# Attention and mixture of experts in one kernel: tail masks over all rows, gate halves exchanged on GpSimd, another order of every engine

## The chip, the core and the metric

The kernel runs on one core of a Trainium2 chip. A core has five engines that run their own instruction queues: TensorE (PE; its weight loads are listed apart as PEld), VectorE (DVE), ScalarE (ACT), GpSimd (POOL) and SyncE (SP), which here only issues DMAs. Engines wait for each other through semaphores, and each works strictly through its own queue: an instruction that waits holds all that stand behind it. The metric is the device time of one execution, in microseconds.

## The reference, cut to what matters

Eight batches of 576 positions. First, attention with 8 heads of 64 in a causal window of 128 positions with a linear bias:

```
rel = pos[:, None] - pos[None, :]
scores = scale * q @ k.T - slope[h] * abs(rel)
attn = softmax(where((rel >= 0) & (rel < 128), scores, -1e9)) @ v
```

The heads' results, side by side, are `x` (576 x 512 for each batch). Then a mixture of four experts, each one a causal attention of width 64 over `x`:

```
logits = x @ w_gate; the two largest of four are kept, w = softmax of these two
for e in range(4):
    y_e = softmax(causal(scale * (x @ wq[e]) @ (x @ wk[e]).T)) @ (x @ wv[e]) @ wo[e]
    out += where(e is kept, w, 0) * y_e
```

## The kernel before

Heads are worked in pairs: a batch has four pairs `g`, each with its heads in partitions 0 to 63 and 64 to 127 of one tile. 576 rows are four blocks of 128 and a tail of 64. For a pair, `attn_s` (line 401) multiplies scores on PE into PSUM, DVE masks and biases them and takes the row minimum of the negated scores (`softmax_block`, a custom DVE instruction), ACT exponentiates with a running sum (`exp_block`), DVE sums and inverts, and POOL or ACT scales the rows (`normalise`, line 467). PE then turns the blocks by transposes against an identity (`attn_t`), and multiplies with v (`attn_pv`). The result is split into a rounded part and a remainder (`rnd`, `ssub`), so that the projections run in the fast float32 form on three products. For each batch, `vproj` (687) makes the experts' values and the gates' logits `lg`, `gates` (726) the gate weights `w`, `qkproj` the queries and keys, `moe_s`, `moe_norm` (835), `moe_t` and `moe_pv` the experts' attention, `moe_wo` the output.

The first four pairs of batch 0 take another road: `fetch` (329) brings only their first 256 rows at first ("the first row fetches": eight DMAs of 128 KB, two for each pair), `first_blocks` scores them against tables `FT` (the tile `KKm` in the rows), and `half_s`, `half_tail` (527) and `half_t` do the rest later. The tables are made at the start from `tbt` (one DMA on ACT's queue) by DVE and POOL. Before that data comes, PE runs eight matmuls on a zeroed tile (`warm`, `AHTm` in the rows).

Two odd exchanges of partition halves run through this: in blocks with odd number, `moe_s` puts the lower 64 rows into the upper partitions. So the logits of odd blocks are copied to `lg` in two halves by DVE (lines 721 to 724), and the tail's gate weights are copied by DVE in `moe_norm` to a column `r[:, 1:2]`. The tail mask `mkt[:, P:]` serves the 64-wide tail blocks, one half of partitions at a time (425, 426).

The order of the work is not that of the code. Everything is recorded first; then `plan` (199) reads `ORDER`, a packed list of numbers, and emits the recorded operations in that order, on every engine; where an operation has two forms (`evac`: ACT or DVE; `rnd`: POOL or ACT; `scl`: POOL or ACT; `ssub`: DVE or POOL) the number also chooses one. `place` then gives the tiles their slots by first use. All instructions are therefore booked to line 1225.

Of the kernel before, what the change touches and what calls it, by code (L numbers as in the profile page):

```python
# [21 lines left out]
E = 4  # L22
# [21 lines left out]
    "4BG=Sx4)*E2XVv$_q7D_SSbM{5}U6*3L>dE25bs}Sx%=UH<17azeXiC}}(8OW2{ld|E3?<P9F@b}Bj2*dCUA_o8?C8J#`8ZU`Xso5QF$;<4$bGPOM(I05;"
    "sfR>JMVW~ysl=1$xt&_De-H^8s1AK)dZa{+pVtz}wO!eR(_DBEKrU^*2mA=CX$G50FYO<Ka2)5nv`yn1XtD#*6ub4=E+A@UG0u-}ug}i0VH<Iu20Os_>>B"
    "zexg%>y#wu<gG?xT*fCt59c`B-coVKJQS@?X@t{$#txLV{IXNo5%)Qvq^?Rx-;DUb}Xxt;(W?Dk%O9_a1^8pOS&?B2IO_lZx1yYwe7CPgcQ<iHlXdBOAL9"
    "{`-bvI-ETCVH}x)^Q$vzi-!c4Jm3EzIwL$MzgbcjTAro;>&M_#3m^(yfY;3%THAr@qzS$Rt*gWKm6$XUjEbz(pN%V@)h%wa;N~fP<_EXEqMB4J*Ok$lv@g"
    "e13ik!d;j#pN?ygK%5GKswYF`ikkJ6UvGBB(bnAN9ZIp{fwYWU+A6Y;7{eQpptCHNk8yDWp_==nE>}zj$P})jx7`YREi(j%iuU?JV-D$x{a}q^8BSU9fCP"
    "~Jf`<|Qxc0m>WsVIf$etvmJM)nJ$?&xfE3_}O%=vSpbe;nQo^8A%m0yd|7rmhj9w^J2cgNATLQ?0G*bO?~pW?g}%j$i%tl!DNmzRp~l<ygLYYI-U_%H+&s"
    "ml3ft33I#jH7(b_izWEr^GpByJFO$TD|gpB`_9%@-3|*1b2@F{B4^GP%`3fa$^=?m7**jFcx~V*^x^l2Nsyn@g-~nD5(=}O*6bm~8G#!JvD>gpavGaj);H"  # L50
    "lAgy_jQB?ild#8D2Q>ki^1%?G6=9$0j>oQXzzJLJj+Nx~WAM%=*q!t#{_859z~tdL+&vo^d3@=8)H<Us}{8nphoTJ+-&zVrf0``-6Uz8Du&5OE<k1gog06"
    "rhBcknTxME7+hZq5uP1e(8CUY;?0vEJP3(IDVOXWzc|$I5j?&*75P*)fZuI{P%vjuB`#I&uq2>Ol+>hBuo`%+X}PWYUris>Gg4NiQjgS{t~`EuyW%%^7PB"
    "dA(JcDWW}y5q3J1QQHG7N4kM|B8l{q5xc0{D>BB+vywkQ;ncN5uiF2SM24;jEAR|hN4t;Yrmi9$qY1jHl!NJ~*oU|+$h*+h3*cOFr+HUOK+P{Emw{*&9?H"
    "IE^ZruU07k>r1V7^6qk2E9^TfIILT+>OAcBf-<1$P%!Ifz}+?AnmiHtdiSGH3{%WDlf58|}w?Nw9V1prY?acHU;Hy96+%yilUZD>0D~8cO9GD6IhL6Zq9P"
    "1$gdGZEwr0)23j3A)_F#q-lh}=r3Nf5gE~4+a9zECu8c_Ef`=JZR}k9+aTAy>yha<_&O5~S*K+8Gby@%J2+Ie{qt*bkK=UAs3guPANY~yQBQ`ot~u%Qc^A"
    "p6i~xv?S%7(1K=jVVXuiNYM3+ks5|V|LIKYmq^muUEwBjOLc7IUGetgDa?oB9NSggGUq`E()^Fs9tiBF)~wdFO?6KGyxm-fW80tD=uyn<rT+No~z%J8<00"
    "4}b@!W(C58mVXv*vNEQaqR`bwq_ejb)vN~y>pC=SGWneV9PHoDUS;(I&GU!735N)Ya3iRYA`*uxgWaHqd!AFdp$Oxjs<&~<R;3h9Rrzy<l>>&L`j6qS^B}"
    "$IAy<qkwKU(%gUvQUC7IXN!gJLIk!u8+)KlPH1@e>>tjD4h~!63%}f?Urb7o>7Rp(Tw^twfDcBp_Y@s5^AZT2HQWy(@66qYQ08Hx+#_;s*C_wNUeBcYgSD"
    "+Z}C|5Qn6m*c4o|oGI({r#4aYTOF+Ox7qP+es?&Qf$oeiha7e}LuhqK{UVqOb1m!1ZfNap$%J-@LBiuy&>1(W|uK2HDmkH&mCWq|~*vwsb&wCDd#$osR99"
    "&aWXYRVr!gUFs**Kr<c#yl`iD^;iX>9{b7LKRq_6yPn#5033QE49=y*Qsif(B$6m+drL%T4(r`3m%kIsns~B1hP?LlzNaj2CEOF6zxN+6MNBW*GG@N<k@1"  # L60
    "A&B*i%kYn8$A)F*U+LB{EfigOFkra$>j1%C9shI0>v#iPln6!w`5(JW4?L<QPUo5a4@8y!`UG8wJpJo|=1`B9Ux<J7woiAK<fS~4;D^yg7U=@7d!&F!SWZ"
    "NSh=`*%6P5!;7iBHOk~%C;=6RNJWJR4EvWuFb>WozhYg|LUg*^+3iXXy1C6zyz%%0Yy)T#4>=D#TC%0h9=wQlj)LEx$Ttq<7VTc<Fa9u?s{aftRpKH%13H"
    "p?K7VodGY0JkP8*6c-WRZPY!g4)2$vLU2%i1OhMjBaV)fC9A(-N4g9yBwUyNnTM@Zd4OO*p2kLUuCa`O@8M+$>tIpig^h;L|gO0Mg1QX6M9GP@uk8E{C;l"
# [1249 lines left out]
```

## Time and profile before

| | |
|---|---|
| median of 3 runs | 476.78 us (476.32 to 477.31) |
| the profiled execution | 477.15 us, of which 475.4 us from its first to its last instruction |
| PE busy | 464.1 us, 98% |
| DVE, ACT, POOL busy | 400.8, 364.8, 240.9 us (84%, 77%, 51%) |
| matmuls and transposes on PE | 7100 |

The page cuts the span into 40 slices of 11.9 us; PE's row there is 7 tenths in the first, 6 in the last, and 9 in all between. The chain of work that ended last is made of PE for by far the greatest part. A time "us" at the start of a row counts from the first instruction of the program.

### The profile page before, as it was taken

The numbers are of one execution on the slowest core, as the hardware profiler recorded it, in microseconds if no ns is written. First come the engines' busy times: TensorE is split into PE (matmuls) and PEld (weight loads), VectorE is DVE, ScalarE is ACT, GpSimd is POOL, SyncE is SP. The second block draws the span as 40 slices with busy tenths as digits, with TensorE's granted clock in tenths as the row PEclk, the third lists the DMA queues.
The fourth block names the chain that finished last, engine by engine and source line by source line (L and its number), as shares of the span: only waits on it lengthen the run. The fifth ranks groups of instructions, "written<-read, shape, count | busy, mean of one in ns | idle before, by whom it ended". The sixth has DMA issues, their size and how long they took to land. (4 is left out here: it accounts for less than half of the span.)

```text
span 475.4 us, 18911 instructions
## 1 busy us (share of the span) xinstructions
PE 464.1 (98%) x7100; PEld 404.2 (85%) x7100; DVE 400.8 (84%) x1863; ACT 364.8 (77%) x1375; POOL 240.9 (51%) x449
## 2 busy tenths in 40 slices
PE   7999999999999999999999999999999999999996
PEld 4788889898789888898889988889789898799875
DVE  3899999989997798798997899797996899963972
ACT  3987898878989568687897958889789587743852
...
GB/s 148 288 198 221 173 90 110 6 26 114 21 263 90 3 59 134 156 103 55 56 128 30 142 27 83 252 9 1 161 99 56 36 75 30 91 1 1 4 90 134
DMA packets 28235, 44.75 MB, mean 94 GB/s; under 512 B 7664, under 2 KB 14192, under 8 KB 28144
## 3 DMA queue, kind: packets, MB, share of 16 engines
...
q14 instruction: 35, 0.29, 0.2%
...
## 5 line engine op out<-in xcount | busy, mean ns | idle before, releaser
L1225 ACT COPY w<-ps 128x512 f32<-128x512 f32 (+4 forms) x231 | 94.2, 452 | 43.7 <-PE ps L1225 33.4
L1225 ACT ACTIVATE w<-w,nm 128x128 f32<-128x128 f32 x252 | 98.8, 395 | 15.2 <-DVE nm L1225 13.5
L1225 PE MATMUL ps<-wx,WH 128*128 128x288 f32 (+2 forms) x512 | 107.5, 300 | 0.2
L1225 POOL TENSOR_SCALAR w<-w,mr,w 128x512 f32<-128x512 f32 (+3 forms) x128 | 77.8, 617 | 47.7 <-DVE mr L1225 22.6
L1225 POOL TENSOR_SCALAR w<-w,r 128x128 f32<-128x128 f32 (+1 forms) x166 | 61.8, 385 | 52.7 <-DVE r L1225 23.8
L1225 PEld LDWEIGHTS ps<-wx,WH 128*128 128x128 f32 x512 | 82.1, 189 | 2.7 <-DVE nm L1225 0.6
L1225 ACT ACTIVATE w<-w,mnm 128x384 f32<-128x384 f32 (+3 forms) x128 | 71.2, 558 | 6.4 <-DVE mnm L1225 6.4
L1225 DVE TENSOR_TENSOR w<-ps,tmt 128x768 f32<-128x768 f32 (+2 forms) x92 | 69.3, 776 | 4.8 <-PE ps L1225 4.6
L1225 DVE CUSTOM_DVE_ANT_0 w<-ps,tbt 128x128 f32<-128x128 f32 x272 | 68.5, 284 | 1.6
L1225 PE MATMUL ps<-w 64*64 64x128 f32 (+3 forms) x1200 | 65.8, 314 | 2.4 <-DMA w<-in_hd 2.4
L1225 PE MATMUL ps<-wx,WL 128*128 128x288 f32 (+2 forms) x256 | 67.3, 297 | 0.0
L1225 PE MATMUL ps<-idt,w 64*128 64x64 f32 (+1 forms) x1160 | 61.4, 231 | 2.9 <-POOL w L1225 2.1
L1225 PE MATMUL ps<-w,vt 64*64 64x192 f32 (+3 forms) x1344 | 60.5, 283 | 0.5 <-DMA vt<-in_vd 0.3
L1225 PEld LDWEIGHTS ps<-w 64*64 64x64 f32 x1200 | 49.4, 136 | 13.2 <-DMA w<-in_hd 4.5
L1225 DVE COPY w<-ps 128x128 f32<-128x128 f32 (+5 forms) x115 | 49.5, 451 | 12.9 <-PE ps L1225 11.2
L1225 PEld LDWEIGHTS ps<-idt,w 64*128 64x128 f32 (+1 forms) x1160 | 49.0, 139 | 13.3 <-POOL w L1225 5.6
L1225 PE MATMUL ps<-WH,wx 128*128 128x260 f32 x288 | 59.9, 289 | 0.0
L1225 PEld LDWEIGHTS ps<-w,vt 64*64 64x64 f32 (+1 forms) x1344 | 53.0, 133 | 6.6 <-issue 1.9
L1225 DVE COPY_PREDICATED ps<-mkt,ps 128x256 f32<-128x256 int32 (+3 forms) x180 | 53.4, 316 | 3.2 <-PE ps L1225 1.0
L1225 PE MATMUL ps<-w,w 64*64 64x64 f32 (+7 forms) x1088 | 53.0, 307 | 0.0
L1225 PE MATMUL ps<-KKm 64*64 64x288 f32 (+8 forms) x640 | 51.1, 411 | 0.0
L1225 ACT ACTIVATE w<-w,r 128x128 f32<-128x128 f32 (+1 forms) x122 | 44.0, 395 | 6.1 <-DVE r L1225 4.5
(107 smaller groups left out, 914.1 us busy)
## 6 DMA issues: line engine op xcount, KB each, us to landing
...
```

The costliest lines, as they stand in the source:

```text
L1225: getattr(getattr(tc.nc, e), m)(*a, **k)
```

## The change

The diff has five parts. The tail mask has two column blocks, one for each half of partitions with zeros in the other, so that a masked copy runs over all 128 partitions; `half_tail` has two such copies in place of one. The logits of odd blocks are copied straight, and the halves change places in the product that makes `w` (POOL, three instructions in place of one); the tail's logits are written in one half. `moe_norm` copies the tail's gate weights by POOL in place of DVE. A few POOL memsets zero what is no longer written. And `ORDER` is another list of numbers.

```
 ORDER = (
-    "c-o~|4_GBvb$>JWyt#LGW;4^wYu;<$i@XXA#N7xjSm*~46ch~4LWKkrT8K-82ph2AE)lw5A%PZjX+R-@f`WktTJQr47FtlKupdNFP*y?Nx}<Eg=+f-!Qdz"
...
+    "c-oCw4M1d9b)NU`nRoB*yzYDJJa<NCDx+XPK_P+xg$NZC5-^a0fw)AlprAv91{5kNC@3hTkbnUL1{4xds9?c>VGStQB>@8w6wH!9yK8q9Qr1Ar)?GvIeLw"
...
-    mkt = cp.tile([P, P + D], I32, name="mkt")
+    mkt = cp.tile([P, 2 * P], I32, name="mkt")
...
-            nc.vector.copy_predicated(s[:D, 3 * P : 3 * P + TAIL], mkt[:D, P:], s[:D, 2 * P + D : 3 * P])
-            nc.vector.copy_predicated(s[D:, 3 * P : 3 * P + TAIL], mkt[D:, P:], s[D:, P : P + D])
+            nc.vector.copy_predicated(s[:, 3 * P : 3 * P + TAIL], mkt[:, P : P + D], s[:, 2 * P + D : 3 * P])
+            nc.vector.copy_predicated(s[:, 3 * P : 3 * P + TAIL], mkt[:, P + D :], s[:, P : P + D])
...
-        nc.vector.copy_predicated(s[:, 0:TAIL], mkt[:, P:], s[:, P:TW])
+        for y in range(2):
+            nc.vector.copy_predicated(s[:, 0:TAIL], mkt[:, P + D * y : P + D * y + D], s[:, P:TW])
...
+        if t == 0:
+            nc.gpsimd.memset(lg[:, NQ, :], 0.0)
...
-            nc.vector.tensor_tensor(lg[D:P, t, :], acc[:D, E * D : n], tm2[:D, E * D :], add)
...
-        if t % 2:
-            for y in range(2):
-                nc.vector.tensor_copy(lg[D * y : D * y + D, t, :], acc[D - D * y : 2 * D - D * y, E * D : n])
-        else:
-            nc.vector.tensor_copy(lg[:, t, :], acc[:, E * D : n])
+        nc.vector.tensor_copy(lg[:, t, :], acc[:, E * D : n])
...
-        nc.gpsimd.tensor_tensor(
-            w.rearrange("p e t -> p t e"), ex, ws.unsqueeze(2).broadcast_to((P, n5, E)), mul
-        )
+        wt = w.rearrange("p e t -> p t e")
+        nc.gpsimd.tensor_tensor(wt[:, 0::2], ex[:, 0::2], ws[:, 0::2].unsqueeze(2).broadcast_to((P, 3, E)), mul)
+        for y in range(2):
+            a, z = slice(D * y, D * y + D), slice(D - D * y, 2 * D - D * y)
+            nc.gpsimd.tensor_tensor(wt[a, 1::2], ex[z, 1::2], ws[z, 1::2].unsqueeze(2).broadcast_to((D, 2, E)), mul)
...
-                nc.vector.tensor_copy(r[ps, 1:2], w[ps, 2 * k + pr, 4:5])
+                nc.gpsimd.tensor_copy(r[ps, 1:2], w[:D, 2 * k + pr, 4:5])
...
+        nc.gpsimd.memset(mkt[:, P:].bitcast(F32), 0.0)
...
-    nc.sync.dma_start(mkt[:, P:], mk[:, P:])
+    nc.sync.dma_start(mkt[:D, P : P + D], mk[:D, P:])
+    nc.sync.dma_start(mkt[D:, P + D :], mk[D:, P:])
```

The two lists hold the same matmuls, transposes and dummies for PE, 4939 instructions in each program. On the recording level DVE goes from 1415 to 1371 operations, ACT from 930 to 917, POOL from 445 to 507, SP from 243 to 244: the edits above account for 52 fewer on DVE and 57 more on POOL, and 13 operations with two forms that were ACT's go to DVE (8) and POOL (5).

The first place is the head of SP's queue, at the start of the program. `w100` and `w101` are the tiles of the first row fetches, `ku4` to `ku6` small pieces of the keys of pairs 4 to 6, `mts` a mask table of the experts' scores, `vt` values, `w51` a piece of the projection weights. Before:

```order
L1225 DMA ku4_148<-in_hd 64x64
L1225 DMA ku5_151<-in_hd 64x64
L1225 DMA ku6_156<-in_hd 64x64
L1225 DMA mts_110<-in_mt 64x512 x2
L1225 DMA w100_91<-in_hd 64x2x256 x4
L1225 DMA w101_92<-in_hd 64x2x256 x4
L1225 DMA w100_91<-in_rd 128x2x320
```

And now:

```order
L1227 DMA w100_91<-in_hd 64x2x256 x4
L1227 DMA w101_92<-in_hd 64x2x256 x4
L1227 DMA w100_91<-in_rd 128x2x320
L1227 DMA w100_91<-in_hd 64x2x256 x2
L1227 DMA vt0_125<-in_vd 128x256
L1227 DMA w100_91<-in_hd 128x2x128
```

The five DMAs ahead of the fetches are gone from there; they stand behind the whole first group, as the 28th DMA of the queue and later.

The second place is POOL's queue at the start. `tbt` is the table from the DMA, `KKm` the tables of the first blocks. Before:

```order
L1225 MEMSET AHTm_123 128x256
L1225 ISA
L1225 TENSOR_SCALAR KKm_122<-tbt_107 128x2x128
L1225 TENSOR_SCALAR KKm_122<-KKm_122 128x512 x2
L1225 TENSOR_SCALAR tbt_107<-tbt_107 128x640
L1225 TENSOR_SCALAR KKm_122<-KKm_122 128x512
```

And now:

```order
L1227 MEMSET AHTm_123 128x256
L1227 MEMSET mkt_106 128x128
L1227 MEMSET lg0_143 128x4
L1227 ISA
L1227 TENSOR_SCALAR tbt_107<-tbt_107 128x640
L1227 TENSOR_SCALAR KKm_122<-tbt_107 128x2x128
L1227 TENSOR_SCALAR KKm_122<-KKm_122 128x512
L1227 TENSOR_SCALAR tbt_107<-tbt_107 128x640
```

One scaling of `tbt` stands ahead of the first table now, and two short memsets ahead of both.

The third place is POOL's queue where it scales pair 5 (`w52` with `r5`). `WOH` is the rounded output weight, made from `w55`, where a DMA puts `wo`; `wx4` is the split of pair 4's result, `w56` and `w53` pair 6. Before:

```order
L1225 TENSOR_SCALAR w52_84<-w52_84,r5_0_158 128x128 x3
L1225 TENSOR_SCALAR WOH_113<-w55_87 128x1024
L1225 TENSOR_SCALAR w52_84<-w52_84,r5_5_159 128x128
L1225 TENSOR_SCALAR w52_84<-w52_84,r5_0_158 128x128
L1225 TENSOR_SCALAR wx4_81<-w20_100 128x512
L1225 TENSOR_TENSOR wx4_81<-w20_100,wx4_81 128x512
```

And now:

```order
L1227 TENSOR_SCALAR w52_84<-w52_84,r5_0_158 128x128
L1227 TENSOR_SCALAR w52_84<-w52_84,r5_5_159 128x128 x4
L1227 TENSOR_SCALAR w52_84<-w52_84,r5_0_158 128x128 x4
L1227 TENSOR_SCALAR w53_85<-w53_85,r6_0_164 128x128
L1227 TENSOR_SCALAR w53_85<-w53_85,r6_5_165 128x128
```

`WOH` no longer stands between pair 5's rows; it comes more than fifty instructions later, behind the first batch's experts' rows. POOL takes nine of pair 5's rows in place of five.

## Rows read from the trace of the kernel before

**Rows 1.** The page, busy time by engine: us (share of the span) xinstructions

```profile
PE 464.1 (98%) x7100; PEld 404.2 (85%) x7100; DVE 400.8 (84%) x1863; ACT 364.8 (77%) x1375; POOL 240.9 (51%) x449
```

**Rows 2.** Table of stretches: window, its length, busy time of each engine

```profile
core 0: us, PE busy (x) PEld busy (x) DVE busy (x) ACT busy (x) POOL busy (x), PEclk, DMA share, GB/s
...
5.40:8.80 3.40, 1.82 (x20) 0.83 (x20) 1.00 (x6) 0.99 (x4) 2.25 (x4) 1.00 0.67 190
8.80:12.20 3.40, 3.40 (x42) 2.20 (x42) 2.05 (x15) 2.68 (x11) 0.46 (x2) 0.50 0.78 239
12.20:16.00 3.80, 3.60 (x58) 2.61 (x50) 3.76 (x23) 3.80 (x17) 2.92 (x8) 1.00 0.94 260
...
58.00:464.00 406.00, 403.71 (x6349) 355.24 (x6347) 351.78 (x1611) 318.74 (x1192) 210.07 (x389) 1.00 0.28 76
```

**Rows 3.** Timeline of the start: start, duration, engine, what [idle before <-releaser]

```profile
1.10 3.78 PE L1225 MATMUL ps<-AHTm 128*128 128x512 f32 x8 [1.10 <-POOL AHTm L1225]
3.16 0.29 DVE L1225 TENSOR_SCALAR KKm<-tbt 128x256 f32<-128x256 bf16 x1 [2.20 <-DMA tbt<-in_tb]
3.21 0.50 POOL L1225 TENSOR_SCALAR KKm<-tbt 128x256 f32<-128x256 bf16 x1 [2.17 <-DMA tbt<-in_tb]
...
5.67 0.72 POOL L1225 TENSOR_SCALAR tbt<-tbt 128x640 bf16<-128x640 bf16 x1
6.75 0.44 PE L1225 MATMUL ps<-w 64*64 64x128 f32 x4 [1.87 <-DMA w<-in_hd]
7.68 0.41 ACT L1225 ACTIVATE w<-w,nmA 128x128 f32<-128x128 f32 x1 [4.76 <-DVE nmA L1225]
```

**Rows 4.** Timeline of SP, the head of its queue

```profile
0.73 1.87 SPq L1225 DMA_DIRECT2D ku<-in_hd  x3
2.65 1.24 SPq L1225 DMA_DIRECT2D mts<-in_mt  x2
3.93 5.20 SPq L1225 DMA_DIRECT2D w<-in_hd  x8
```

**Rows 5.** Waits: who waited for whom, us in total, times, longest

```profile
PE ps L1225 <- DMA w<-in_hd: 2.4, 3, 1.9
PE ps L1225 <- POOL w L1225: 2.1, 5, 1.1
DVE mr L1225 <- POOL w L1225: 5.3, 4, 2.7
```

**Rows 6.** Timeline of PE at 25 to 27 us

```profile
25.93 1.37 PE L1225 MATMUL ps<-w 64*64 64x192 f32 x28 [0.34 <-DMA w<-in_hd]
```

**Rows 7.** Timeline at 54 to 58 us, POOL and PE

```profile
55.47 1.04 POOL L1225 TENSOR_SCALAR WOH<-w 128x1024 fp32r<-128x1024 f32 x1 [2.74 <-DMA w<-in_wo]
...
56.48 0.72 POOL L1225 TENSOR_SCALAR w<-w,r 128x128 f32<-128x128 f32 x2
...
56.91 1.13 PE L1225 MATMUL ps<-idt,w 64*128 64x64 f32 x17 [1.09 <-POOL w L1225]
```

**Rows 8.** Timeline of the end, PE and the last copy

```profile
466.60 0.96 PE L1225 MATMUL ps<-WOH,ALm 128*128 128x512 f32 x3 [0.22 <-POOL ALm L1225]
...
471.82 0.37 ACT L1225 COPY w<-ps 128x256 f32<-128x256 f32 x1 [1.58 <-PE ps L1225]
```

**Rows 9.** Groups by shape: xcount | busy us, mean ns of one | idle before

```profile
L1225 POOL TENSOR_TENSOR ALm<-w,AHm 128x512 fp32r<-128x512 f32 x13 | 16.7, 1287 | 8.6 <-ACT AHm L1225 8.1
L1225 POOL TENSOR_TENSOR w<-ex,ws 128x20 f32<-128x20 f32 x8 | 1.8, 230 | 13.7 <-DVE ws L1225 7.9 <-DVE mr L1225 5.8
...
L1225 DVE COPY_PREDICATED ps<-mkt,ps 64x64 f32<-64x64 int32 x56 | 12.6, 229 | 1.2
L1225 DVE COPY mr<-w 64x1 f32<-64x1 f32 x32 | 4.6, 143 | 3.1 <-POOL w L1225 2.7
L1225 DVE TENSOR_TENSOR ALm<-w,AHm 128x512 fp32r<-128x512 f32 x3 | 2.8, 937 | 0.0
L1225 DVE COPY_PREDICATED ps<-mkt,ps 128x64 f32<-128x64 int32 x4 | 0.9, 224 | 0.0
```

More of the change, by code (lines that the diff above doesn't have):

```diff
@@ L44 @@
[L44 to L63, printed above, removed]
@@ new lines @@
+    "TVuGN7V-rV=@-#Op;&UY>*&ZNC=1Nu@Dr$!TE6VeLkb%+f_gv1yk_b!R4qU^GhOgW|tt;#_Guq4}>u@sg_Pz3BnAq9Q?^YWCv@vi5~rJ8c7ju3(g!XwZLS"
+    "cE)OIy)>o5D~Hc96~eaCR5s%wm`gyDq62Y`&~SwbSPNC;b4E{uD@@1F@>bg0}dzKrQBy~>XCJ<x5r8zd4K*<^O}T2utv&POQ9k!)OG*!d1xEA)pvpL?b#l"
+    "jXerFIlBO9Des0HNeZ(%Ddb0O(Z@&Enbm!B;c*=La*Len}ViOc;dIgrx*_Y2X!X}!r+AWI1h2Put&=x+xrAi*%dk)z0pkT9TAE0FzU?@L37c9U%<$UX#pM"
+    "?K0Kh=xofFNfgMr3jA3Y>SrS%5P40E`6IRMx~p0v#iHb~*)8;KH_L+3AR0fOP0eZh!Vin=lgFRKHZ5buJGA>hiM3hV$LIsRxrNb@g0{f(LVxBI*7~0Fu{1"
@@ new lines @@
+    "_|uwlIRIe$0ys%@TDyhJfZb|`3lN{Q5fW={ZEX=HRJ&Rdys(#&oOTG_R~*D<Su;l<)+*-WE&}_eT(Z1VPxq50&W)`Wi+E24X{x`cJUStyIwS%T4`Ooz^Rv"
+    "bMn%0iStb)GgTv9%m16UD*T@Ke380rV;>!u@jKs$6;p{`n{Uu;fWR$H(#y+7OC)+~)p=cG#_MFWxo0b~n^7$WdeNO(vsoW;L>dBK5OvK4BSc&tdd+xziJB"
+    "=)+x+)G;#3PoFhjPN{`Z6c9yM1H(ONsZ1Zt%?g++v3gyq=dr3=H9iW7`4X{eYbYN!c21pH7$LA4ZfN|+p=8=)EAHy6ddF@=z-SOkG*S+)I!yRybKD)Zng6"
+    "b3qe-8xHJD-?4BU?iOJ$j($^o&tO_U^0~nubhm5kxj91<PkxfNihDB3937@aO*tax&5Gar46hS_b8t^{#b@0_4cE5vy-a;gM&i>HFRi%$RIZ48Q`ZFj7aF"
@@ new lines @@
+    "+p;L*$@3OiyB7VceJB8EmDF97lc7F=~-dd<hqokO#ii)Tz)7S);^W=pE|r>rAMu_~9Mll?}DTfx51n4m*RapFT}mLdj!~m$^3p=3x#l4#C_xx)m}Cm*xS^"
+    "FU&2#jX7AD%+DNx>)DXA*qD*(p1qM-SJ`m+QxDEY-@!))xu~tjTiQ`y*j#5*Wk+47(oUltEXCaDR~pg7=JUl3rTEknP(TpLMIlP4YzuQJPTWW&AOsxQ&_a"
+    "QI@yet-BRN5KMF-`P0RXGjh3f_{;;y68k~CNksm7v=l_l}|fn{1Mq#>20Gzd>x9G3J#;!MrRwxsOK3$E&v&aqX%n=QRJVrox*0bj1Mq~Ma)s;R^xgk0A8C"
+    "w>VpKi>K`KLF@w=IiW%5rFi*31-ZI+jt1JpO*2d|9%|;2+9~$K?!i?QTmtkTj}QrvpYF(o_-yPvX!*y?kr<S_*~LshI=&}?p_8p+%|XcBpD$@zJL#$_&T|"
@@ new lines @@
+    "=Wiwe6%S%6c{eKUxUqg?5u_JTWC)#EPAtM$bZBhL;Xn%^IKzrb@V~Z@&KmZ96+AYep(vm#)8ZIb-dg}aHa)g!^Gtp*rw;eAm_u+)bwjJ0lMOCn;T%TRWLo"
+    "qv-ubbMshX9hcNZI<@2#OXS9({WB8JrS{u|kgIfx(VuaG3UQ1WCi?IH>2KetWOAnxtd`WTeuSB(dcr1cpFjMtqovR_damkn%D$QiX^_DY|3qbjaNezx|_Q"
+    "gFRSU0Z>Uk|67+$hN<io=O4b|?B2f67qHaPT;Y_IKm0mgu~-Q0m;!g2xn~mg;&!g4u25n;ETQ<O5ovnUTVAA7KE9<KY?0Z01<tGXu;)3g@RNU=n+S`FU4("
+    "`&J`-Jg`ZMyk*B_NQxX0?evc(=+vr^WKr=Fr20|SKBCr3p~NixdJh)luhh-{cLGSmB-4ik$*O#q0X5U5Sfu*NNIT;DA+4W=FCuW#BgB<+(iSaeDV$<Kbz{"
@@ new lines @@
+    "i$bv_zJoRbi;upNWxOkIM7&`t|$d4bf91I)`8~Ym}_WodMzuEgv4aqd!Ku1D(7-#PU`46l2l$&kgzU`vo=RaOk{XaH*7*%b6a&_)K2dT+*wljSlW`hzeyb"
+    "hecGR2RGeu9XsB(V*Uf3HB|DcBfaMh-OF;1jj;K%Gp_GMdPoKee0DBVV0}JP8)F#4xe|X>@c)PU`LLe9*2&OJ<!`3A?48bf2uhIs9P=NeZXW&(k&~|sz;="
+    "(juUL&*9zuNp=F*@6qo|artgY$wgOwR{q6g+)fXq@|j7he4J=VqS;Tmkofb85ORTAfUQ7f_m2>>X&XYVK$zU9HxR<`RiW@h$N6dp`KB6tY=bL4ncPQ%a+G"
+    "wd;cH#E@}zYP`XV{<Ge!6AhI36|sGxKUZ-m1$lEJMI{ltmunhfx0f0P>dITJp;&2bD?!l*czBldihU{BbSq~;$${C>jiOTFogs<fRElx~ayH#tEy8z$KJj"
@@ new lines @@
+    "6Zbp88%9SDbDhwD#Is8dPWj6ne*Z+(knP;6<32#Vh1Ft{$0>8KOWLl^``p!UKCJ{E|yS78fYge5!v)eFz@IO#)o=Z!-qWa;bAnl2d|&ZuoWOFkI;8mNgRm"
+    "wpr!cN4L*$NJSrQL|<)`D^W6jeYr$*9(2)!sA;D7Jx-DI%1`6FsiD&3Lp`Z;;Hwi8enUnt~zduPBGp)(3=(8Mv>hfSNF;{<K7$hh4oFi&<DaNZIp@ST)bR"
+    "WU0g=y088KkY()y)UVAQNmX?$%A<Juls0g5~9v99}pM~5^xfV4+B@!p>c&w6SxM)J#7jZY^zA1*rx(f^C=jcj`nnI@K*|FA@;CV=ek@%$WN6O5d+iR_B*K"
+    "L#AsAbqLJ@GQB@p@9l^E$+?;W;USy#Gl@r+sy${-CIKAg!a{b*-!gn%iIk#<i!1Rj_tN!X5X+8=j<IhWCB9ApH74+&P#AK|rJxXs(WJfw5us^QK2^(gf+0"
@@ new lines @@
+    "@vE;D3!kN3XS@5l`{t;cfekvTYF*lippr?L8lPf`w|6oR=P7XNtx;jYV$jLooV6fj$(=o0ZKoi1=XNe&aS(>6BC=jw65Nlsqk`NN`v<-T_3;bOp;NWJ11W"
+    "G2-I~w^J6CsOqhb>*h{%x=0jo3P0EFK)T~0c5>077SkMXo@ku#H%Qm2OQcimrsYMT_?x^aFZvA3(;UhHhd&Z^q}q58H?Mr^ZM$HkTPgS`#s&Pa7<b69b;b"
+    "^AA8$-V(FM)!p;jYHGi#$Hsq>qceW@Fi<vF-aAE@U{=;!E{=(HOQ8OTA_0HUid+Me&;Cu>8A>6S}%X$EvG+q*N-|Jtz9vTs{@l)*W_P3&rq5MsT7u~0?Tf"
+    ";%1E?=l9KST-z+}=KkLfc?qzYgaXz5Hy_O%fi8?o#3jiiYClPt(c4z)shl@;PS5^?H{?q$PsIWgtQ^aS93^-C_A&HkQ!t*PK-{fcVqkv|Nl0lj{hnSPEn~"
@@ L112 @@
+    "RfPj#_{-`KSkv#`izN;rt41-UkS}i+$*YrB_3{suLQgNqV(}I8Ozk(SWBO<_z*s-=N7jHE7tTKqFS9Y7a9;o@xpGf5&gy$m|@3&COWpc=V`(#A3k$I!05R"
+    "Nh5Nz&H(Ct&Wwy&TcbF3L<9zPd+I(qui1N)V;GgYDdp+D_DU{4+EGs}c-=NWy}UxqdywW2O5`bNJVS9BF!Vb<1&L~J<ipZPL#6%;I-`Qm(Ug%Tyu!t(%Q="
+    "rU*9v$25KYgf48|%-bs({SBXI`GSb1y|q*|HdVR?2Qs{WdNkI#HJtbg@61Mw|p{b_@{CCB?5rU<km^FZ8lRLcDo$GtrNSDy_39}m9<*8"
 )
```

91 lines of the change are left out of this document (40 added, 51 removed).

## The prediction

> **What bounds the kernel now.** I read the page first: PE is busy 98% of the span, DVE 84%, ACT 77%, POOL 51% [rows 1]. So the time is PE's, and a change in DVE, ACT or POOL is worth what it takes out of PE's idle time. That is 475.4 - 464.1 = 11.3 us, and the table of stretches says where it lies. In the 406 us from 58 to 464 PE lacks only 406.00 - 403.71 = 2.3 us [rows 2]. The rest, 9 us, is at both ends: 1.10 us before the first dummy matmul and 1.87 us before the first score [rows 3], 1.1 us at 57 us [rows 7], and at the end about 3.6 us after the last matmul, which is the last copy out of PSUM at 471.82 [rows 8] with its DMA. The list of waits gives the names: the largest for PE are the row fetches (2.4 us, three times) and POOL's scaled rows (2.1 us) [rows 5]. PE's busy time also holds short stalls that lie under matmuls still running, since ends of matmuls are modelled; no row prices them, and they are the largest unknown of any new order.
>
> The change has the same matmuls for PE in nearly the same sequence of stages. I take PE's own work as unchanged, and look for the waits that go, one by one, against the profiled execution (477.15 us; 0.37 above the median of 476.78).
>
> **The start.** SP's first five issues, three of `ku` and two of `mts`, take from 0.73 to 3.89 us, and only then the first row fetch is issued, at 3.93 [rows 4]. The first score starts at 6.75, that is 2.82 after that issue, and PE idles 1.87 before it, having finished its dummies at 1.10 + 3.78 = 4.88 [rows 3]. With the five gone from the head the fetch is issued at 0.73, 3.20 earlier, and its data is there at about 0.73 + 2.82 = 3.55. PE is then held by its own dummies until 4.88. So the first score gains all of the 1.87, and no more at once. What is late next? The first softmax needs the tables: DVE's, two short instructions from 3.16 on, and POOL's, which now comes after a scaling of `tbt` of 0.72 and is ready at 3.21 + 0.72 + 0.50 = 4.4 [rows 3]: still before the scores, so that displacement costs nothing; if the table's DMA is slowed by the fetches that now fly with it, there is about 1 us of room.
>
> After that the stage is no longer PE's. The fetches come 0.65 us apart (8 in 5.20 [rows 4]), and the scores between 5.4 and 12.2 us wait for them; ACT starts its first exponential at 7.68 [rows 3] and is busy 0.99 us until 8.80 and 2.68 of the next 3.40 [rows 2], so it idles 0.13 + 0.72 = 0.85 for lack of data. From 12.2 on DVE and ACT are full (3.76 and 3.80 of 3.80). With the data 3.2 earlier, ACT starts 1.87 earlier and could lose its 0.85 of idling, 2.7 in sum. The bounds: 1.87 if only PE's first wait goes, 3.20 if everything slides with the queue. I take 2.4, somewhat under ACT's sum. Against it stand four additional tail masks on DVE in a full stretch, 4 x 0.224 = 0.9 us [rows 9]; that is why I stay under.
>
> [...]
>
> **The second fetch wait.** At 25.93 PE idles 0.34 for another row fetch [rows 6], part of the second group's fetches. They stand earlier in the queue now, by the five and by two more. I take 0.3, between 0 and 0.34.
>
> **The output weight on POOL.** At 55.47 POOL starts `WOH` after 2.74 us of waiting for the DMA of `wo`, and behind it stand two scalings of pair 5's rows; PE's transposes of them start at 56.91 after 1.09 idle [rows 7]. In the new order `WOH` stands more than fifty instructions later, with its data long there. The wait of 1.09 goes, unless the sums of pair 5 come just as late: these rows take 0.72, so without `WOH` they could be done before PE asks. Bounds 0 and 1.09; I take 1.0.
>
> **The end.** PE waits 0.22 for POOL's `ALm` at 466.60 [rows 8]. In the new order DVE makes it, in 0.94 where POOL takes 1.29 [rows 9], 0.35 less: 0.2 goes. After the last matmul the same copy and the same DMA follow; nothing changes there.
>
> **The edits themselves.** The tail masks: 64x64 took 229 ns, 128x64 takes 224 [rows 9]; nothing. On DVE 52 instructions of some 0.15 us go, 32 of them the copies `mr<-w` of 143 ns, and with the four masks this leaves DVE about 7 us lighter over the span; the waits of DVE for POOL's weights go too (5.3 us [rows 5]). PE waits for DVE hardly at all, so I count 0, and 1 us at the most. POOL gets 57 more small ones. The nearest row is `w<-ex,ws` at 230 ns [rows 9], which makes at most 13 us on an engine that idles half of the time; their cost to PE is 0 while POOL is ahead, and a rival below where not. [...]
>
> **Waits that are drawn anew.** The remaining waits from 58 to 464, 2.3 us, depend on small distances between instructions, and every one of them is drawn again. I expect the same sum, and allow 1.5 either way, which also stands for the stalls inside PE's busy time.
>
> **Sum.** 2.4 + 0.3 + 1.0 + 0.2 = 3.9. From 477.15 that is 473.25; from the median of 476.78 it is 472.9. I say 473.1.
>
> **Rivals.**
> [...]
>
> Second, the order gives it back. The start gains, but the new order leaves PE some 3 us more short waits between 58 and 464 than the 2.3 it has: 476.5, no change that can be told. For it: DVE stands at 352 of 406 us in that stretch [rows 2], so that a row at the wrong place of its queue is quickly late for PE. Against it: the edits make DVE lighter, and PE's sequence of stages is nearly the old one.
>
> Third, slower: POOL becomes late. The product for the gate weights waited 13.7 us on POOL before, for DVE [rows 9]; it is three instructions now, and copies follow, all in the same queue as the scalings that PE's transposes need. When POOL was held 2.74, PE lost 1.09 [rows 7]. Once in each of eight batches makes 8.7: 477.15 - 3.9 + 8.7 = 482.0. From four batches on (4.4) it is more than the gain. [...] Against it: POOL idles half of the span, and before it waited as long at the same place with no such loss for PE.
>
> Fourth, the change does nothing at the start: another DMA or table holds the first score where it was, near 6.7. Then 1.5 is left: 475.3.
>
> **How the numbers follow.** The forecast has 0.58, the first rival 0.17, the second 0.11, the third 0.07, the fourth 0.07. A measurement of this kernel can tell about 0.2%, 1 us, from no change. Faster by more than that, under 475.8, are the forecast, the first and most of the fourth: 0.81. The same: the second and a rest, 0.12. Slower: 0.07. The range goes down by the upper bounds of the front (0.8 more), and of the new waits (1.5): 470.8. Up it takes in the first and fourth rivals and part of the second: 476.0.
>
> **What would show it.** SP's first row is the fetch; PE's first score starts near 4.9, with no row of 1.9 us of waiting for `in_hd`; POOL's first scaling and the first transposes come 2 to 3 us earlier. No wait of POOL for `in_wo`. DVE's busy time falls by some 3 to 7 us, POOL's rises by about 10. PE's busy time in the middle, per 100 us of work, stays as it is. I am wrong if PE's first score is still near 6.7, if the middle stretch takes some 3 us more than now, or if PE's waits for POOL exceed 5 us in the list.

## The result

The changed kernel takes 464.73 us (median of 4; 464.07 to 464.96) where the kernel before, beside it on the same chip, takes 477.04 (476.32 to 477.77): ratio 0.974 [0.9721, 0.9758], 12.3 us. Faster was forecast, but by 3.9, and 464.73 lies 6 us below the range.

The page of the changed kernel, busy time by engine, answers to [rows 1]:

```profile
PE 456.4 (99%) x7100; PEld 399.8 (86%) x7100; DVE 389.0 (84%) x1819; ACT 360.1 (78%) x1362; POOL 252.9 (55%) x511
```

Its span is 463.0 us. PE idles 6.6 us in place of 11.3: that is 4.7 us, about the size of the forecast. The rest, 7.7 us, came out of PE's *busy* time, although the matmuls are the same 7100. So the busy time held stalls; the 12.3 us gained are more than all the idle time that PE had.

The table of stretches after (columns as in [rows 2]) and the start:

```profile
5.40:8.80 3.40, 3.40 (x58) 2.27 (x56) 2.87 (x20) 2.80 (x13) 2.79 (x5) 1.00 0.81 228
8.80:12.20 3.40, 3.08 (x38) 1.77 (x34) 3.37 (x21) 3.40 (x17) 2.88 (x7) 1.00 0.93 266
12.20:16.00 3.80, 3.80 (x46) 3.18 (x38) 3.64 (x21) 3.55 (x13) 3.37 (x8) 1.00 0.98 324
56.00:450.00 394.00, 392.45 (x6301) 346.89 (x6299) 335.78 (x1546) 313.28 (x1168) 221.37 (x444) 1.00 0.29 79
```

```profile
0.73 5.35 SPq L1227 DMA_DIRECT2D w<-in_hd  x8
...
1.09 3.78 PE L1227 MATMUL ps<-AHTm 128*128 128x512 f32 x8 [1.09 <-POOL AHTm L1227]
...
3.39 0.29 DVE L1227 TENSOR_SCALAR KKm<-tbt 128x256 f32<-128x256 bf16 x1 [2.51 <-DMA tbt<-in_tb]
...
4.80 4.50 PE L1227 MATMUL ps<-w 64*64 64x128 f32 x64
...
6.00 0.40 ACT L1227 ACTIVATE w<-w,nmA 128x128 f32<-128x128 f32 x1 [3.08 <-DVE nmA L1227]
```

The start went as forecast: the fetch heads the queue, the first score is at 4.80 with no wait, the first exponential 1.68 us earlier than in [rows 3], and the stretch from 8.80 to 12.20, with a granted clock of 0.50 in [rows 2], now has 1.00. In the middle a PE record takes 392.45 / 6301 = 62.3 ns where it took 403.71 / 6349 = 63.6 [rows 2]; over 6300 records that is about 8 us (a rough figure: the two windows do not hold quite the same matmuls). Two more places, POOL's output weight (waits for nothing now) and the end (DVE's product in place of POOL's; PE has no wait there):

```profile
95.51 1.05 POOL L1227 TENSOR_SCALAR WOH<-w 128x1024 fp32r<-128x1024 f32 x1
...
454.17 0.69 DVE L1227 TENSOR_TENSOR ALm<-w,AHm 128x512 fp32r<-128x512 f32 x1 [0.49 <-ACT AHm L1227]
```

### The profile page after: what moved, and what is told of

Same layout as the page of the kernel before. It is cut to its first block, busy times and chain, and to the rows that moved or that the text cites. A ratio compares the mean times of both kernels' runs of the same rounds, so it can differ in the third digit from the quotient of the medians.

```text
span 463.0 us, 18918 instructions
## 1 busy us (share of the span) xinstructions
PE 456.4 (99%) x7100; PEld 399.8 (86%) x7100; DVE 389.0 (84%) x1819; ACT 360.1 (78%) x1362; POOL 252.9 (55%) x511
## 4 chain that ended last, share of the span: by engine, by line
PE 88%; DVE 5%; DMA 2%; POOL 2%; issue 1%; SPq 1%; ACT 1%; ACTq 0%; POOLq 0%; DVEq 0%
PE ps L1227 88%; DVE w L1227 3%; POOL w L1227 1%; DMA vt<-in_vd 1%; DMA w<-in_hd 1%; SPq L1227 1%; ACT w L1227 1%; DVE ps L1227 1%; DVE MPL L1227 0%; POOL wx L1227 0%; DVE wx L1227 0%; DVE mr L1227 0%; DVE mnm L1227 0%; DVE r L1227 0%; DVE xq L1227 0%
## 5 line engine op out<-in xcount | busy, mean ns | idle before, releaser
L1227 ACT COPY w<-ps 128x512 f32<-128x512 f32 (+5 forms) x232 | 92.4, 449 | 38.2 <-PE ps L1227 27.9
L1227 ACT ACTIVATE w<-w,nm 128x128 f32<-128x128 f32 x252 | 98.5, 394 | 11.8 <-DVE nm L1227 11.7
L1227 POOL TENSOR_SCALAR w<-w,mr,w 128x256 f32<-128x256 f32 (+3 forms) x128 | 77.8, 617 | 33.2 <-DVE mr L1227 27.0
L1227 ACT ACTIVATE w<-w,mnm 128x512 f32<-128x512 f32 (+3 forms) x128 | 70.9, 556 | 8.2 <-DVE mnm L1227 7.8
L1227 PE MATMUL ps<-w 64*64 64x128 f32 (+4 forms) x1200 | 64.9, 309 | 0.4 <-DMA w<-in_hd 0.4
L1227 PE MATMUL ps<-w,vt 64*64 64x192 f32 (+4 forms) x1344 | 60.1, 283 | 0.8 <-DMA vt<-in_vd 0.6
L1227 DVE COPY w<-ps 128x256 f32<-128x256 f32 (+5 forms) x114 | 50.8, 464 | 10.7 <-PE ps L1227 10.1
L1227 PE MATMUL ps<-idt,w 64*128 64x64 f32 (+1 forms) x1160 | 58.4, 230 | 0.9 <-POOL w L1227 0.7
L1227 PEld LDWEIGHTS ps<-w 64*64 64x64 f32 (+1 forms) x1200 | 49.7, 134 | 10.6 <-issue 1.4
L1227 DVE COPY_PREDICATED ps<-mkt,ps 128x128 f32<-128x128 int32 (+2 forms) x184 | 52.8, 313 | 3.8 <-PE ps L1227 1.6
L1227 ACT ACTIVATION_READ_ACCUMULATOR w<-w,nm 128x1 f32 x252 | 48.0, 190 | 0.0
```

Source lines behind the costliest of these rows:

```text
L1227: getattr(getattr(tc.nc, e), m)(*a, **k)
```

## The experiments

Names: b_ is the kernel before with an edit, a_ the changed kernel with one. A ratio is to the kernel before, run beside it (476.7 to 477.5 us).

| run | us | ratio |
|---|---|---|
| b_head: five DMAs behind the first fetches | 475.08 | 0.9966 [0.9946, 0.9985] |
| b_head_woh: and `WOH` later | 474.90 | 0.9966 [0.9942, 0.9989] |
| b_mr: 32 copies to POOL | 476.92 | 0.9996 [0.9982, 1.0011] |
| b_lg: logits' edits | 474.96 | 0.9958 [0.9940, 0.9977] |
| b_lg_mr | 475.70 | 0.9979 [0.9964, 0.9994] |
| b_mask: tail masks | 470.50 | 0.9865 [0.9830, 0.9901] |
| b_mask_mr | 471.88 | 0.9902 [0.9864, 0.9941] |
| b_edits: all edits, a memset badly placed | 477.93 | 1.0012 [0.9994, 1.0030] |
| b_edits_head_woh | 475.98 | 0.9981 [0.9953, 1.0010] |
| b_edits2: all edits, memset early | 470.20 | 0.9850 [0.9828, 0.9873] |
| b_edits2_head_woh | 468.23 | 0.9811 [0.9784, 0.9838] |
| b_lo: both half masks on the lower rows | 470.44 | 0.9870 [0.9851, 0.9889] |
| b_up: both on the upper rows | 482.49 | 1.0115 [1.0096, 1.0134] |
| a_mr: the 32 copies back on DVE | 476.06 | 0.9981 [0.9963, 0.9999] |
| a_mr_free | 472.60 | 0.9909 [0.9891, 0.9927] |
| a_mr_dump | 465.45 | 0.9756 [0.9724, 0.9788] |
| a_lg: logits' edits undone | 467.50 | 0.9789 [0.9764, 0.9814] |
| a_head: five DMAs back at the head | 467.28 | 0.9800 [0.9785, 0.9814] |

### The front alone, in the old order: b_head, b_head_woh

At the end of `plan` of the kernel before (for b_head_woh `WOH` also goes down to just ahead of `WOL`):

```
+    head = [o for o in out if o[0] == "sync"][:5]
+    out = [o for o in out if not any(o is h for h in head)]
+    at = [j for j, o in enumerate(out) if o[0] == "sync" and named(o, "tmt")][0] + 1
+    out[at:at] = head
```

> The kernel before, with one thing changed: the five DMAs (ku4 to ku6, mts twice) stand behind tmt in SP's queue and the first row fetches at its head. Theory A (the start slides with the queue): 3.0 to 3.7 us less than before, the first score at about 4.9 us, the first transpose at about 9.5. Rival B (only PE's first wait of 1.87 goes, the rest is held by ACT and DVE): 1.5 to 2.4 us less. In both the stretch from 70 to 460 us keeps its length within 1 us.

> The kernel before with the head of SP's queue as in b_head and, on POOL, WOH moved down to just ahead of WOL. If PE's stop of 1.09 us at 57 us is WOH's: 0.8 to 1.1 us less than b_head. Rival: the sums of pair 5 are as late, then it is equal to b_head within 0.3.

The front brought 1.6 us, `WOH` nothing on top. In b_head's trace PE's 200th record starts 1.5 us earlier, its 400th no earlier at all. In between stands one new wait, for another fetch of the second group, and a stretch at the lower clock level, 0.50 (second fence: window, length, PE, PEld, DVE, ACT, POOL busy, clock):

```profile
23.82 3.26 PE L1234 MATMUL ps<-w 128*128 128x192 f32 x34 [2.25 <-DMA w<-in_rd]
```

```profile
24.48:27.89 3.41, 3.41 (x36) 2.55 (x33) 2.06 (x12) 1.97 (x7) 2.49 (x5) 0.50 1.10 224
```

And `WOH` starts on POOL without waiting, since `wo`'s DMA came earlier with the whole queue:

```profile
52.76 1.05 POOL L1234 TENSOR_SCALAR WOH<-w 128x1024 fp32r<-128x1024 f32 x1
```

So the third term needs no move of `WOH`: it lies inside what the front brings, and the two could not be added. How much of the 1.6 us is the front's stays open. In this trace PE's 250th to 600th record start where they did before, behind the place at 57 us PE is 0.6 us ahead, and 0.9 more comes between its 2000th and 4000th record (142 to 269 us), where the edit changes nothing.

### The copies alone: b_mr and a_mr

```
-                nc.vector.tensor_copy(r[ps, 1:2], w[ps, 2 * k + pr, 4:5])
+                nc.gpsimd.tensor_copy(r[ps, 1:2], w[ps, 2 * k + pr, 4:5])
```

a_mr is the other way round, in the changed kernel.

> The kernel before with only the 32 copies of the tail's gate weights made by POOL in place of DVE (one line). Theory D (PE's short hidden waits come from a full DVE, and a lighter DVE shortens them): DVE loses 4.6 us of work and 5.3 us of waits for POOL, the time falls by 1.5 to 4 us. Rival O (the gain in the middle is the new order's, not the edits'): equal to before within 1 us.

> The changed kernel with only the 32 copies of the tail's gate weights given back to DVE (one line). Theory D: 1.5 to 4 us more than the changed kernel (466.2 to 468.7). Rival O: equal to it within 1 us.

In the old order the copies are worth nothing on either engine; in the new one, moving them back costs 11.3 us, three times what the theory allowed. The trace of a_mr shows why: list of waits, then the first of the places (the PE row answers to the two DVE rows), then the stretch behind it (columns as above):

```profile
DVE mr L1227 <- POOL w L1227: 14.5, 11, 3.3
```

```profile
127.83 0.15 DVE L1227 COPY mr<-w 64x1 f32<-64x1 f32 x1 [1.87 <-POOL w L1227]
...
129.11 0.14 DVE L1227 COPY mr<-w 64x1 f32<-64x1 f32 x1 [1.14 <-POOL w L1227]
...
130.91 0.53 PE L1227 MATMUL ps<-wx,WH 128*128 128x288 f32 x2 [2.48 <-DVE w L1227]
```

```profile
131.65:135.06 3.41, 3.41 (x28) 3.13 (x28) 2.05 (x16) 3.17 (x12) 2.10 (x2) 0.50 0.16 61
```

A copy of 64 numbers stands at the head of DVE's queue and waits for POOL; behind it stands the copy out of PSUM that PE needs, and PE stops for 2.48 us. Then 3.41 us with a granted clock of 0.50 follow, on matmuls that fill all of it. This happens at 131, 291 and 407 us.

### Wait or load: a_mr_free, a_mr_dump

Both have the 32 copies on DVE, but not the source that POOL makes (tail rows get a constant for their gate weights). The second also writes where nobody reads:

```
-                nc.gpsimd.tensor_copy(r[ps, 1:2], w[:D, 2 * k + pr, 4:5])
+                nc.vector.tensor_copy(r[ps, 1:2], idt[ps, 0:1])          # a_mr_free
+                nc.vector.tensor_copy(dump[ps, 0:1], idt[ps, 0:1])       # a_mr_dump
```

> The kernel after, with the 32 small copies for the tail's gate weights on DVE at the same places of its queue as in the run that put them back there, but read from a constant tile in place of POOL's product w (so the tail rows of the experts are scaled by a constant instead of their gate weights: that part of the computation is left out). DVE thus has the same 32 instructions as in that run, and does not wait for POOL's w. Theory B (what cost 11.3 us was DVE standing at a copy that waits for POOL, and everything queued behind it): 464.0 to 466.5 us, as the kernel after, and PE has no visible idle of over 1 us behind the first 20 us. Rival L (DVE's load of 32 more instructions, or POOL's relief of them, moves the time): 470 to 476 us. In between both have a part.

> The kernel after, with 32 copies of a 64x1 constant on DVE at the places of the queue where the run that put the tail's gate weights back on DVE had them, written to a tile that nobody reads, so they wait for no other engine, neither for the product w nor for a reader of an old tile mr; POOL makes no copies (the tail rows are scaled by a constant in place of their gate weights: left out). The run before this one still had DVE waiting 10.4 us in 8 waits for POOL at these copies, and lost 7.9 us; with the waits for w it was 14.5 us in 11 waits, and 11.3 us lost. Theory B (DVE held in its queue by these waits is what costs): 464.0 to 466.0 us, as after. Rival L (32 more instructions of 143 ns on DVE, 4.6 us, cost PE about their length): 468 to 470 us. DVE's waits mr for POOL's w are expected under 2.5 us, as in the kernel after.

The first missed: it still waits, which the edit was to prevent. With the tile `mr` out of the way the wait is gone too, so it was most likely for a reader of the tile's earlier content. Waits of DVE in the changed kernel, in a_mr_free and in a_mr_dump:

```profile
DVE mr L1227 <- POOL w L1227: 1.6, 2, 0.9
```

```profile
DVE mr L1227 <- POOL w L1227: 10.4, 8, 2.2
```

```profile
DVE mr L1228 <- POOL w L1228: 2.1, 2, 1.4
```

By accident this is a series of doses: DVE held 1.6, 2.1, 10.4 and 14.5 us (a_mr) gives 464.7, 465.5, 472.6 and 476.1 us. In this series each microsecond in which DVE is held costs PE some 0.9 (the stretches with a granted clock of 0.50 behind the stops are in it), while 32 instructions that wait for nobody cost 0.7, which is within the noise:

```profile
L1228 DVE COPY dump<-idt 64x1 f32<-64x1 f32 x32 | 4.7, 146 | 0.6
```

Theory B stands, rival L falls. The 0.9 is no price for every wait of DVE: in the old order the same wait is 5.3 us [rows 5], in b_mr it is 2.9, and nothing was gained.

```profile
DVE mr L1225 <- POOL w L1225: 2.9, 3, 1.5
```

### All edits in the old order: b_edits, b_edits2 and with the front

All edits of the change, each new instruction where the old one was. In b_edits the memset of the tail's logits stood just ahead of the first block's copy (and in batches where the tail's logits are written before, it wipes them); in b_edits2 right behind the last reader of the tile's earlier content:

```
+            if t == 0:                                   # b_edits
+                nc.alt["pre"][id(nc.ops[-1])] = [("gpsimd", "memset", (lg[:, NQ, :], 0.0), {})]
...
+    for b, m in enumerate(ms):                           # b_edits2: ms, these memsets
...
+            at = 1 + max(j for j, o in enumerate(out) if any(lgof(x) == lgof(ms[b - 1][2][0]) for x in o[2]))
```

> The kernel before with all edits of the change (tail masks over all rows, straight copies of the logits, halves exchanged in POOL's product, the tail's weights copied by POOL, the memsets) but its own order: each new instruction stands where the one was that it replaces, or right behind it. Theory O (the middle 7 us come from the new order; the edits alone are worth nothing): 475.7 to 477.5 us. Rival E (the edits, by DVE's 7 us of lighter work, bring the middle's gain in whatever order): 469 to 472 us. PE's time from 58 us to its last record, 406 us before, is expected at 405 to 407 by O, and at 400 to 402 by E.

> The kernel before with all edits, its own order, and in that order the five DMAs put behind the first row fetches and WOH put down to just ahead of WOL: all that the prediction named, without the rest of the new order. Theory O (the rest of the order, not any of these, makes the difference to the kernel after): 473.5 to 475.5 us, that is 9 to 11 us over the kernel after. Rival E (edits and front together): 465 to 469 us.

> The kernel before with all edits in its own order, as in the run b_edits, but with the memset of the logits' tail early on POOL, right behind the last reader of the tile's earlier content (there DVE waited 5.1 us in two waits for that memset, which the change itself does not have). Theory O (the middle's gain is the new order's): 473.5 to 476.5 us, at most the 1 us by which PE's stalls for the memset count, and 1 us of DVE's lighter work. Rival E (the edits bring the middle's 7 us, and the memset hid it): 468 to 472 us.

> The same (all edits in the order of before, the memset early), with the five DMAs put behind the first row fetches and WOH down to just ahead of WOL. Theory O: 472 to 475 us, which leaves 7 to 10 us of the difference to the kernel after to the rest of the order. Rival E: 465 to 469 us.

By b_edits the edits were worth nothing, and theory O looked proved. But its trace shows DVE waiting 5.1 us in two waits for that memset; here are the sum and the second:

```profile
DVE ps L1248 <- POOL lg L1248: 5.1, 2, 3.0
...
216.08 0.11 POOL L1248 MEMSET lg<- 128x4 f32 x1
216.22 0.18 DVE L1248 COPY ps<-lg 128x20 f32<-128x20 f32 x1 [2.13 <-POOL lg L1248]
216.90 0.27 PE L1248 MATMUL ps<-idt,w 64*128 64x64 f32 x1 [0.87 <-DVE w L1248]
...
217.87 0.90 PE L1248 MATMUL ps<-idt,w 64*128 64x64 f32 x14 [0.69 <-ACT w L1248]
```

With the front and `WOH` (b_edits_head_woh) it is no better than b_head alone. A memset of 0.11 us behind POOL's scalings holds DVE 2.13 us. Without it the same edits in the same order bring 7.2 us (0.985 of 477.04), and the front and `WOH` another 1.9. Theory O falls in its main part. What is left for the rest of the order is 468.0 - 464.7 = 3.3 us, by the two intervals give or take 1.6.

### Which edit: b_lg, b_mask, b_lg_mr, b_mask_mr

The edits of b_edits2 in parts: masks (mask), logits (lg), copies (mr), each with the rest of its edit as in the change:

```
+            nc.vector.copy_predicated(s[:, 3 * P : 3 * P + TAIL], mkt[:, P + D :], s[:, P : P + D])    # mask
...
+                nc.vector.tensor_copy(lg[:, t, :], acc[:, E * D : n])                                 # lg
...
+                nc.gpsimd.tensor_copy(r[ps, 1:2], w[ps, 2 * k + pr, 4:5])                             # mr
```

> The kernel before, its order, with the logits' edits alone: straight copies of odd blocks (16 fewer copies on DVE), the tail's logits once (8 fewer), halves exchanged in POOL's product (3 instructions for 1), the memset early. Theory A (the edits add up, each by what it takes off DVE: logits 24 of 60 instructions): about 473.5 to 475.5 us. Theory P (the logits' edit is the one that counts): 469.5 to 472 us. Theory N (only together): 476 to 478 us.

> The kernel before, its order, with the tail masks over all rows alone (56 masked copies of 64x64 become 128x64, four more in the half_tail steps). By the rows of the kernel before, 229 against 224 ns each, it takes nothing off DVE: theories A and P 476.5 to 478 us. Rival M (the masks are what counts, by a wait that the two half copies had and the full ones don't): 470 to 474 us.

> The kernel before, its order, with the logits' edits and the tail weights' copies on POOL, without the masks. Theories A, P and N: 469.5 to 471.5 us, as with all edits. Rival M: 474 to 477 us.

> The kernel before, its order, with the masks and the copies on POOL, without the logits' edits. Theories A, P and N: 475.5 to 477.5 us, as with the copies alone. Rival M: 470 to 474 us.

The masks are what counts, the rival that I thought least of: 6.2 of 7.2 us (476.66 - 470.50). The logits bring 1.7 alone; the copies on POOL nothing, or on top of the masks a loss of about 1, which the intervals leave open. Yet a masked copy in b_mask takes 224 ns in place of 229 [rows 9]:

```profile
L1243 DVE COPY_PREDICATED ps<-mkt,ps 128x64 f32<-128x64 int32 x64 | 14.1, 224 | 0.2
```

### Why the masks: b_lo, b_up

```
-            nc.vector.copy_predicated(s[D:, 3 * P : 3 * P + TAIL], mkt[D:, P:], s[D:, P : P + D])
+            nc.vector.copy_predicated(s[:D, 3 * P : 3 * P + TAIL], mkt[:D, P:], s[:D, 2 * P + D : 3 * P])
```

That is b_lo; b_up replaces the lower copy by the upper. Each leaves out the mask of one half of the tail rows.

> The kernel before with the tail mask's copy on the upper partitions replaced by a second one of the lower partitions (the mask of the upper 64 rows of the tail blocks is left out): 56 copies of 64x64 as before, all on partitions 0 to 63. Theory U (an instruction on the upper half alone does not overlap with its neighbours on DVE, about 0.22 us each, 28 of them 6.2 us, and PE pays for them): 470 to 472 us, and nearly all 56 copies start before the end of the instruction ahead and take about 215 ns. Rival N (any copy of 64 partitions stands alone, or the two waits of the half copies count): 475.5 to 478 us.

> The same the other way round: both copies on the upper partitions (the mask of the lower 64 rows is left out), 56 on partitions 64 to 127. Theory U: 56 copies that stand alone in place of 28, 6 us more on DVE: 480 to 484 us, less where DVE has slack at these places. Rival N: 475.5 to 478 us.

Theory U, in both: -6.4 us without the 28 copies on the upper half, +5.6 with 56 of them. (Of b_up's excess its trace, of an execution of 483.35 us, has 1.5 us by PE's 200th record, at 27.68 against 26.17, while its first copy of this kind comes at 38.90; that leaves some 4 to 5 us to the edit.) The same 56 copies of 64x64, by groups, in b_lo and in b_up (before: 229 ns, half of each kind):

```profile
L1225 DVE COPY_PREDICATED ps<-mkt,ps 64x64 f32<-64x64 int32 x56 | 11.8, 214 | 0.1
```

```profile
L1225 DVE COPY_PREDICATED ps<-mkt,ps 64x64 f32<-64x64 int32 x56 | 13.2, 240 | 1.7
```

The mean duration shows only 26 ns of it. The rest is in the starts. One copy between two softmax instructions, on DVE, in b_lo and in b_up (start, duration):

```profile
92.93 0.28 DVE L1225 CUSTOM_DVE_ANT_0 w<-ps,tbt 128x128 f32<-128x128 f32 x1
93.14 0.08 DVE L1225 DVE_READ_ACCUMULATOR2_ANT nm<- 128x1 f32 x1
93.14 0.22 DVE L1225 COPY_PREDICATED ps<-mkt,ps 64x64 f32<-64x64 int32 x1
93.27 0.27 DVE L1225 CUSTOM_DVE_ANT_0 w<-ps,tbt 128x128 f32<-128x128 f32 x1
```

```profile
97.45 0.28 DVE L1225 CUSTOM_DVE_ANT_0 w<-ps,tbt 128x128 f32<-128x128 f32 x1
97.67 0.08 DVE L1225 DVE_READ_ACCUMULATOR2_ANT nm<- 128x1 f32 x1
97.78 0.24 DVE L1225 COPY_PREDICATED ps<-mkt,ps 64x64 f32<-64x64 int32 x1
98.03 0.29 DVE L1225 CUSTOM_DVE_ANT_0 w<-ps,tbt 128x128 f32<-128x128 f32 x1
```

In b_lo the copy starts before the instruction ahead has ended (93.14 against 92.93 + 0.28), and the next one 0.09 us before the copy's end: from softmax to softmax 0.34 us. In b_up each waits for the end of the one ahead: 0.58 us. The 0.24 between them, 28 times, is 6.7 us, near the 6.4 of b_lo and more than b_up shows. Of all 56 copies, 46 in b_lo have a follower that starts before their end, 3 in b_up, 22 before.

PE pays for it where it waits for the minimum `nm` behind the mask (PEld's waits, of the kernel before, b_lo and b_up: us, times, longest):

```profile
PEld ps L1225 <- DVE nm L1225: 2.7, 11, 0.4
```

```profile
PEld ps L1225 <- DVE nm L1225: 0.9, 4, 0.4
```

```profile
PEld ps L1225 <- DVE nm L1225: 5.8, 19, 0.6
```

and most of it hides in PE's busy time, which goes from 464.1 [rows 1] to 458.9 in b_lo and 469.2 in b_up:

```profile
PE 458.9 (98%) x7100; PEld 403.5 (86%) x7100; DVE 395.8 (84%) x1863; ACT 363.4 (78%) x1375; POOL 241.1 (51%) x449
```

```profile
PE 469.2 (97%) x7100; PEld 405.3 (84%) x7100; DVE 405.7 (84%) x1863; ACT 365.5 (76%) x1375; POOL 240.5 (50%) x449
```

### Undone in the new order: a_lg, a_head

a_lg copies odd blocks in two halves again, writes the tail's logits twice and has one product for `w`; a_head puts the five DMAs back:

```
+        if t % 2:                                        # a_lg
+            nc.vector.tensor_copy(lg[:D, t, :], acc[D:, E * D : n])
+            nc.alt["post"][id(nc.ops[-1])] = [("vector", "tensor_copy", (lg[D:, t, :], acc[:D, E * D : n]), {})]
...
+    out[at:at] = back                                    # a_head: back, the five DMAs; at, SP's first
```

> The kernel after with the logits' edits undone and its order kept: odd blocks copied to lg in two halves by DVE (the second right behind the first), the tail's logits written twice, one product for w on POOL; 24 more small instructions on DVE, 24 fewer on POOL; the tail masks and the tail weights' copies stay as in the kernel after. Theory B (small instructions on DVE that wait for nobody cost little): 464.5 to 466.5 us. Rival L (each costs its length, 24 x 0.15 = 3.6 us): 467.5 to 469 us. Rival T (the new order holds only with all edits): 472 us and more.

> The kernel after, with the five DMAs (three of ku, two of mts) put back at the head of SP's queue, ahead of the first row fetches. In the order of before the same five DMAs, taken from the head, brought 1.6 us. Theory S (the start is worth more in the new order, because its other queues are written for early fetches; the shift of the whole queue counts): 467.3 to 468.5 us, that is 2.6 to 3.7 us over the kernel after, and PE's first score at 6.7 us. Rival H (as in the old order): 465.8 to 466.8 us. [...]

a_lg costs 2.8 us, between its theories; half of it is there by PE's 200th record, in the start, where no logits are made, so how much of the 2.8 is the edit's stays open. a_head costs 2.55, what theory S expected at its lower end: SP's head and PE's first score are as before again.

```profile
0.74 1.86 SPq L1238 DMA_DIRECT2D ku<-in_hd  x3
...
2.64 1.24 SPq L1238 DMA_DIRECT2D mts<-in_mt  x2
3.92 5.20 SPq L1238 DMA_DIRECT2D w<-in_hd  x8
...
6.61 0.43 PE L1238 MATMUL ps<-w 64*64 64x128 f32 x4 [1.84 <-DMA w<-in_hd]
```

## Why the prediction was right in sign and wrong in size

**The start: right.** 2.4 us were forecast, and a_head prices it at 2.55 in the new order, where POOL's first scaling comes 2.8 us and the first transpose 3.2 us earlier than before. That b_head got only 1.6 from the same move shows that the term is not the head's alone: the old order had a wait of 2.25 us for a later fetch in store, which the new one does not have.

**The clock: no loss by it.** The 0.17 of the first rival rested on 1.7 us as the price of the lower clock level (0.50 from 8.80 to 12.20 before [rows 2]) on transposes. No run shows that price: all four executions of the changed kernel have a mean granted clock of 1.000, and what the level costs where it does come, these runs do not settle. Three executions of a_head with a mean of 0.996, in its trace by a stretch of 3.41 us at 0.50 from 7.92, took 467.11 to 467.39, the one with 1.000 took 467.65: no cost that shows. In b_head_woh, where the stretch stands at 24.89, behind a wait for a fetch, the three with 0.996 took 475.99 to 479.31, the seven others 473.30 to 475.31. Behind stops in the middle, b_edits took 476.28 in the execution with 0.999 and 478.18 to 478.91 in those with 0.988 (an estimate from that mean: three such stretches, as a_mr's trace has with 0.989), some 0.7 us each, but 476.46 in the one with 0.993. The stop ahead of each stretch is part of all these differences.

**The second fetch wait: right**, it is gone from its place. **The output weight: counted twice**, as b_head shows; 1.0 should have been 0. **The end: right** as to PE's wait of 0.22, which is gone; no run prices it alone.

**The edits: the step that failed.** "The tail masks: 64x64 took 229 ns, 128x64 takes 224; nothing" compared durations, and "PE waits for DVE hardly at all, so I count 0, and 1 us at the most" read PE's waits from its visible idle time. Both are wrong, and the first is a 6 us error. What a masked copy took of DVE's time shows in the starts: between the same two softmax instructions 0.34 us on the lower half in b_lo, 0.58 on the upper in b_up, where the overlap is lost on both sides. Upper copies in b_up start 33 ns behind the end of the instruction ahead (median, accumulator reads left aside), where lower ones in b_lo start 75 ns before it: a hold of 0.11 us. The side behind shows in the medians of before and after: the follower of a 64x64 copy (half of each kind) starts 31 ns behind its end, that of a 128x64 copy in the changed kernel 91 ns before it. Two holds of 0.11 us a copy, 28 copies, make an estimate of 6.2 us. The logits' half copies, which read one half and write the other, look alike: before, 30 of 32 have a follower that starts behind their end, and their edit brought 1.7 us for 24 instructions of about 0.155. Why DVE holds such an instruction was not shown.

The second sentence failed because PE's stalls on DVE are not idle time in the profile. The prediction named them "the largest unknown of any new order" and then gave them 1.5 us; PE's busy time fell by 7.7. The rows to read were PEld's waits, 11 of them for `nm`, and DVE's starts.

**The waits drawn anew: missed.** The rest of the order is worth 3.3 us, where 0 within 1.5 was forecast. The traces do not show where it lies: the changed kernel is ahead of b_edits2_head_woh by 1.4 us at PE's 200th record (22.60 against 24.03), not at all at the 250th (28.48 against 28.34) and by 2.2 at the last, and the two orders of PE's records differ. Which of its moves bring the 3.3 was not tried.

**The sum.** Edits 7.2, front and `WOH` in the old order 1.9, rest of the order 3.3: 12.4, where 12.3 was measured. The 3.3 is what the other two leave, so the sum is no test of them. The third rival (POOL late) had its place wrong and its mechanism right: not PE but DVE is held by POOL, and a_mr and b_edits show a price of 11.3 and 7.7 us. The change escapes it because POOL itself makes the copies that need its product and the memsets stand early.

**Of the signs named beforehand** those of the start all came, POOL's busy time rose by 12.0 us (10 forecast), DVE's fell by 11.8 where 3 to 7 were forecast (its 52 instructions had the four masks taken off already: 56 go and 4 come), and PE's busy time in the middle, which was to stay, fell: the two that point at DVE.

Open: why the copies, moved to POOL in the old order, bring nothing although they include 16 on the upper half. They are cheap in the new order too: of the 32 in a_mr_dump only 7 have a follower that starts before their end, and all together cost 0.7 us. So a hold on DVE is not dear everywhere; it may be so only where PE soon waits for what stands behind, as behind the masks, but this was not tried. In b_mr's trace the middle is 1.1 us shorter and the start 1.6 longer. b_up's start is 1.5 longer as well, ahead of anything that its edit changes, which speaks for chance.
